# RWKV-7 and a GELU network in one kernel: turning the block inverses of two chunks on VectorE instead of through DRAM, with a new order of steps

## The chip, the cores and the metric

The kernel runs on one core of a Trainium2 chip. The metric is the device time of one execution in microseconds (us); a comparison uses the median of several runs. A profile is taken by the hardware profiler in an execution of its own. Its span is the time from the core's first to its last instruction.

## What is computed

Two parts follow each other. The first is a recurrence over 768 time steps, for 4 batches and 8 heads, each with a state of 40 x 40; the second is a two-layer network with the exact GELU on the 3072 x 320 rows that come out.

```python
# r, k, v, w, a, b: (4, 8, 768, 40) float32
for t in range(S):
    y[:, :, t] = einsum('bhd,bhde->bhe', rt, state)
    Sa = einsum('bhde,bhe->bhd', state, at)
    state = state * wt[:, :, None, :] - einsum('bhd,bhe->bhde', Sa, bt) + einsum('bhd,bhe->bhde', vt, kt)
x = y.transpose(0, 2, 1, 3).reshape(3072, 320)
h = x @ w_in                                  # w_in: (320, 2048), in 64-bit words
out = (0.5 * h * (1 + erf(h / sqrt(2)))) @ w_out   # w_out: (2048, 320), in 64-bit words
```

## The kernel before

**Chunks.** The 768 steps are cut into 12 chunks of 64 (c = 0 to 11). Inside a chunk the recurrence is written as matrix products, so that only one 64 x 64 triangular system per batch and head has to be inverted; the state is passed from chunk to chunk. The 32 pairs of batch and head lie on 128 partitions in pairs, 16 matrices side by side in the free dimension, two halves of 64 partitions, each of two blocks of 32.

**Steps and engines.** Every piece of work is a small function marked `@step`, named by two or three letters. The string in `order` lists all steps of all chunks in the order in which their instructions are issued; `perform` calls them one by one. There is no other scheduler: each engine executes its own instructions in just this order, and waits at one whose inputs are not there yet or whose target is still being read. So a step that waits holds up what stands behind it on its engine, and on SP's DMA queue too. The five engines are PE (TensorE), DVE (VectorE), ACT (ScalarE), POOL (GpSimd) and SP, which only issues DMAs.

**One chunk.** `Lw`, `La`, `Lb`, `Lk`, `LV`, `Lr` load the inputs (SP). `lg`, `wT`, `cu`, `ec`, `ew` form the cumulated decays; `ta`, `tb`, `tk`, `tr`, `tv` turn the inputs, on PE for chunks 0 to 2 and on DVE from chunk 3 on. `nm` (PE) and `nk` (DVE, line 839) make the strictly upper triangular matrices N; `vm`/`vk` and `am`/`ak` two further masked products. `av`, `xm`, `xc0`, `xc1` form the right-hand side, `sm` (PE) applies the inverse, `sc` masks it, `pk`, `pb` update state and output, `oa`, `om`, `od`, `oc`, `ot`, `tn` scale the state, turn it for the next chunk and write the network's input `xt`; `ox` moves rows of `xt` between partitions by DMA.

**The inverse.** For chunk 0 it is made of repeated squarings (`qt`, `qi`, `qm`, `qz`, `qb`, `qa`, `qc`, `ql`, `qx`), a chain between PE, DVE and ACT. For all other chunks the diagonal blocks of 32 x 32 (64 of them) are inverted on GpSimd by substitution, and then joined to the 64 x 64 inverse:

- `Ns` writes the blocks of N to DRAM, `Nl` reads them back so that each partition holds one whole block (1024 numbers in `Nb`), twice, once for each half of the partitions: one half solves the even rows of a block's inverse, the other the odd rows.
- `iz` sets `W` to rows of the identity, `ic.c.j0.j1` (lines 901 and 903) takes steps j0 to j1 of the substitution: a product into `tmp` and an addition to `W`, 62 instructions a chunk. Eight such steps make a solve.
- `Is` writes the inverses to DRAM, `If` reads them back as diagonal blocks into `Tt`, `Ij` some of them into `T2`.
- `tc_` (DVE, line 1001) turns them, `jm`, `jc`, `km`, `kt0`, `kt1` compute the block off the diagonal.

**The network.** `mh.c.p` (PE, line 1241) multiplies 256 rows of `xt` by 128 columns of the first weights, `ge` is the GELU, and the second product is made in one piece for chunk 0 (`pm`) and by seven half-size products with sums for the others (`m1` to `m7`, `s1` to `s4`, `e1` to `e6`, line 1280).

**The weights.** They come as 64-bit words (`Lf`, `Lf5`, `Ls`) and are made 32-bit numbers in 26 units u: 0 to 9 of 128 x 512 for `w_in`, 10 to 25 of 128 x 320 for `w_out`. `cp`, `cm`, `cs` (DVE) and `ce` (ACT) take exponent, mantissa and sign apart; the last step is either `cv` (two instructions on DVE, lines 612 and 613), or `cl` and `cn` (ACT, lines 620 and 627) with `cg` (two on GpSimd, lines 635 and 636), or, for unit 2 alone, `cx` (two matmuls on PE) with `cy`.

**Warm steps.** `warm` and `warm_first` are matmuls whose result nobody reads.

Of the kernel before, what the change touches and what calls it, by code (L numbers as in the profile page):

```python
# [16 lines left out]
def order(chunks, first_seven):  # L17
    return """
        pads_rows.0 Lw.0 sums_mask lg.0 pads_w.0 wT.0 of_half_set identity pads_r.0 ew.0 Lf.1.0.0 pads_r.1
        pads_extra.3 pads_VR.0 pads_a.0 cu.0 ec.0 Lk.0 pads_w.1 pads_a.1 bias_set pads_extra.0 first_ones.1  # L20
        first_ones.0 Tt_zero onward_set Lb.0 sb.0 La.0 warm.4.25 tb.0 pads_VR.1 sk.0.p pads_extra.2 upper_mask
        warm.4.14 tk.0 sn.0 ta.0 sa.0 warm_set warm.4.16 nm.0 nk.0 qt warm.4.5 Lf.3.1.0 Lf.1.1.0 Lf.0.0.0
        Lf.3.0.0 Lf5.0.1 Lf.0.0.1 cp.1 cm.1 Lw.1 La.1 ce.1 cs.1 qm.0 lg.1 qi.0.p pads_extra.1 qi.1.v qz.0
        qb.0.0.v cv.1 Lf.0.1.0 Lf.0.1.1 cu.1 qb.0.1.a qc.0 wT.1 ew.1 cm.3 cp.3 ce.3 ec.1 qm.1 qz.1 qb.1.1.a qc.1
        cp.0 ce.0 cl.3 cl.5 cn.3 Lr.0 Lb.1 Lf.2.1.1 Lf5.1.0 cs.3 qa.1 warm_first ta.1 qb.1.0.v sb.1 sa.1 kc.0
        qm.2 qz.2 cs.0 qb.2.0.v cm.0 tr.0 qc.2 rc.0 qa.2 cg.3 am.0 tb.1 qb.2.1.a cp.5 cv.0 cm.5 sn.1 qm.3 nm.1
        qz.3 nk.1 qa.3 qb.3.0.v ce.5 cn.5 Lf.1.1.1 LV.0 qb.3.1.a tv.0 Lf5.0.0 Lf.2.1.0 Lf.2.0.0 Lf.2.0.1 Lf5.1.1
        LV.1 Ns.1.1 Ns.1.0 Ls.0 Ls.1 Lf.1.0.1 Lr.1 Lk.1 cs.5 cm.2 cp.2 ak.0 qm.4 qa.4 cg.5 cp.7 ql vc.0 cl.7 cl.2
        vm.0 cn.2 cx.2 warm.4.11 vk.0 qc.3 ce.2 cs.2 cy.2 cp.4 ce.7 qx cm.4 cm.7 ce.4 cn.7 Ls.2 Lf.3.0.1 Lf.3.1.1
        Nl.1.0 Lw.2 Ls.4 Nl.1.1 av.0 jm.0 jc.0 km.0 xc1.0 cs.7 pads_rows.1 cg.7 cs.4 cv.4 cp.6 xc0.0 kt0.0 kt1.0  # L30
        ce.6 cm.6 cl.6 cn.6 cp.9 cm.9 tr.1 cs.6 ce.9 rc.1 sm.0 sc.0.1 cs.9 sc.0.0 cv.9 tv.1 pk.0 pb.0 cg.6 cp.8
        sk.1.v om.0.0 cm.8 od.0.1 od.0.0 om.0.1 ce.8 vc.1 cs.8 cv.8 cp.10 tk.1 kc.1 am.1 oc.0 ot.0.0 warm.4.15
        vm.1 ot.0.1 Ls.3 Ls.7 ce.10 lg.2 Lr.2 ox.0.1 Lb.2 La.2 tn.0 cm.10 cs.10 ak.1 cp.11 cv.10 wT.2 cu.2 ew.2
        ce.11 vk.1 cp.12 tr.2 ec.2 ce.12 rc.2 cs.11 cm.11 cv.11 cm.12 cs.12 cm.13 cp.13 cv.12 cp.14 cm.14 av.1
        ym.1 yc.1 sb.2 warm.4.1 xm.1 ta.2 ox.0.0 Ls.6 Ls.5 Ls.8 Ls.9 La.3 Lw.3 tb.2 ce.14 xc1.1 ce.13 sn.2 sa.2
        cs.14 cv.14 cs.13 cp.16 ce.16 cv.13 cp.15 ce.15 xc0.1 mh.0.2 nm.2 mh.0.6 cs.16 cm.16 cm.15 cs.15 cv.15
        cp.17 cm.17 nk.2 ce.17 cv.16 cp.18 ce.18 cs.17 cv.17 cp.19 ce.19 cs.18 cm.18 cm.19 Ls.11 LV.2 cs.19 cv.19
        mh.0.7 mh.0.4 mh.0.3 mh.0.0 ge.0.1 cp.21 ce.21 cm.21 cv.18 Ls.10 Ns.2.1 Ns.2.0 mh.0.1 tv.2 mh.0.5 iz.1
        ic.1.0.4 ic.1.4.8 ic.1.8.12 ic.1.12.16 ic.1.16.20 ic.1.20.24 ic.1.24.28 ic.1.28.31 unused.v unused.a
        Ls.13 Is.1.0.s Is.1.1.s Nl.2.0 Ls.15 Ls.12 Nl.2.1 iz.2 ic.2.0.4 ic.2.4.8 ic.2.8.12 ic.2.12.16 ic.2.16.20  # L40
# [1360 lines left out]
```

## Time and profile before

| what | value |
|---|---|
| median of 3 runs | 667.89 us (666.51 to 668.05) |
| the profiled execution | 671.35 us |
| its span | 669.6 us |
| mean granted clock of TensorE | 0.977 |
| instructions | 28037 |
| packets of DMA, bytes | 306133, 79.23 MB |

All shares and durations in the profile belong to the one profiled execution. A row of the timeline gives start, duration, engine, line, operation, what is written and read, the count, and in brackets the idle time before it with what ended it. A row of a group gives the busy time in us, the mean of one instruction in ns and the idle time before. PEclk is the granted clock of TensorE as a share of full speed.

### The profile page before, as it was taken

The page shows a single profiled execution, that of the slowest core. Times are in us where ns is not written, and L with a number is a line of the kernel's source. Part 1 is how long each engine was busy: PE and PEld are TensorE (multiplying, and loading weights), DVE is VectorE, ACT ScalarE, POOL GpSimd, SP SyncE. Part 2 cuts the span into 40 slices and gives each one's busy share as a digit, 9 for nine tenths or more (in the row PEclk, how much of TensorE's full clock was granted, in tenths as well). Part 3 has the DMA queues.
Part 4 walks back from the last instruction along what each step waited for, and adds up shares of the span by engine and source line. Part 5 has one row for each costly group of instructions (what it writes and reads, how often), then busy time and mean ns, then how long its engine had stood idle before and what let it go on. Part 6 is the DMA issues. An engine that isn't in the chain of part 4 may idle for free.

```text
span 669.6 us, 28037 instructions
## 1 busy us (share of the span) xinstructions
PE 632.3 (94%) x12416; PEld 556.7 (83%) x12416; DVE 449.6 (67%) x572; ACT 285.2 (43%) x388; POOL 390.1 (58%) x796
## 2 busy tenths in 40 slices
...
GB/s 149 169 162 180 134 154 192 155 110 111 160 117 100 171 83 143 153 106 164 142 81 147 160 111 114 158 99 122 165 102 132 108 85 131 14 81 9 28 14 20
DMA packets 306133, 79.23 MB, mean 118 GB/s; under 512 B 285628, under 2 KB 300892, under 8 KB 306012
## 3 DMA queue, kind: packets, MB, share of 16 engines
...
## 4 chain that ended last, share of the span: by engine, by line
PE 66%; POOL 13%; SPq 7%; DMA 6%; issue 4%; DVE 3%; ACT 1%; DVEq 0%; POOLq 0%; ACTq 0%
PE bank L1241 25%; PE bank L1280 22%; PE bank L197 18%; POOL W L903 7%; POOL tmp L901 7%; SPq L437 2%; SPq L560 2%; DMA inv_blocks<-W 1%; DMA w_out_sb<-in_moe_w_in_dram 1%; DMA Tt<-inv_blocks 1%; DMA Nb<-N_blocks 1%; SPq L880 1%; DMA SM<-in_w_dram 1%; SPq L527 1%; DMA N_blocks<-spare 1%
## 5 line engine op out<-in xcount | busy, mean ns | idle before, releaser
L1241 PE MATMUL bank<-xt,w_in_sb 64*128 64x256 f32 x1920 | 224.6, 386 | 0.0
L901 POOL TENSOR_TENSOR tmp<-W,Nb 128x126 f32<-128x126 f32 (+22 forms) x341 | 161.7, 474 | 91.5 <-DMA Nb<-N_blocks 56.6
L1241 PEld LDWEIGHTS bank<-xt,w_in_sb 64*128 64x128 f32 x1920 | 184.3, 190 | 24.1 <-issue 1.1
L903 POOL TENSOR_TENSOR W<-W,tmp 128x126 f32<-128x126 f32 (+22 forms) x341 | 165.5, 485 | 26.7
L1280 PE MATMUL bank<-w_out_sb,gt 128*128 128x160 f32 x704 | 102.1, 302 | 0.0
L1246 ACT ACTIVATE gt<-bank 128x1024 f32<-128x1024 f32 x48 | 48.9, 1024 | 122.5 <-PE bank L1241 120.8
L1280 PEld LDWEIGHTS bank<-w_out_sb,gt 128*128 128x128 f32 x704 | 96.6, 190 | 3.9 <-issue 2.6
L1109 DVE TENSOR_TENSOR SM<-bank,upper 128x832 f32<-128x832 f32 (+1 forms) x24 | 23.1, 989 | 20.1 <-PE bank L197 19.9
L1197 ACT COPY conv<-st 32x128 f32<-32x128 f32 (+2 forms) x55 | 28.0, 509 | 16.8 <-DVE st L1191 16.1
L1280 PE MATMUL bank<-extra,conv 128*128 128x160 f32 x208 | 30.4, 300 | 0.0
L1233 DVE TENSOR_TENSOR os<-os,bank 128x160 f32<-128x160 f32 x44 | 13.9, 315 | 23.5 <-PE bank L1280 16.1
L590 ACT ACTIVATE conv<-conv,rebias 128x320 uint32<-128x320 uint32 (+1 forms) x26 | 16.1, 622 | 30.5 <-DVE conv L583 30.3
L1280 PEld LDWEIGHTS bank<-extra,conv 128*128 128x128 f32 x208 | 28.8, 190 | 0.2
L1001 DVE STREAM_TRANSPOSE conv<-Tt 128x512 f32<-128x512 f32 x11 | 7.8, 710 | 31.3 <-DMA Tt<-inv_blocks 31.2
L1050 DVE COPY Tt<-bank 32x512 f32<-32x512 f32 x9 | 6.2, 689 | 33.6 <-ACT Tt L1050 33.6
L696 DVE TENSOR_TENSOR_SCAN kT<-spare,kT 128x256 f32<-128x256 f32 x36 | 24.7, 744 | 4.9 <-ACT kT L689 4.9
L1161 DVE TENSOR_TENSOR st<-bank,st 128x832 f32<-128x832 f32 (+1 forms) x22 | 21.0, 986 | 10.1 <-PE bank L197 10.1
L892 POOL MEMSET W<- 128x512 f32 x11 | 5.9, 537 | 36.7 <-DMA inv_blocks<-W 36.7
L1233 DVE TENSOR_TENSOR conv<-gt 128x1024 f32<-128x1024 f32 x11 | 14.0, 1276 | 19.6 <-ACT gt L1246 19.6
L197 PEld LDWEIGHTS bank<-SM,Tt 64*64 64x64 f32 x768 | 19.2, 140 | 8.6 <-issue 4.5
L1280 PE MATMUL bank<-extra,gt 128*128 128x160 f32 x176 | 26.0, 301 | 0.0
L197 PE MATMUL bank<-SM,Tt 64*64 64x104 f32 (+1 forms) x768 | 22.5, 261 | 3.5 <-ACT Tt L1050 1.2
...
## 6 DMA issues: line engine op xcount, KB each, us to landing
...
```

The lines of the kernel that those rows point to most:

```text
L197: nc.tensor.matmul(o, lhsT, rhs, start=first, stop=True, skip_group_check=True)
L590: nc.scalar.activation(power, power, ACT.Relu, bias=rebias, scale=8.0)
L696: nc.vector.tensor_tensor_scan(logs[:, at:at + n], onward, logs[:, at:at + n], 0.0, ALU.mult, ALU.add)
L901: nc.gpsimd.tensor_tensor(t, W[:, :rows, j:j + 1].to_broadcast([P, rows, rest]), Nb[:, j:j + 1, j + 1:].to_broadcast([P, rows, rest]), ALU ...
L903: nc.gpsimd.tensor_tensor(W[:, :rows, j + 1:], W[:, :rows, j + 1:], t, ALU.add)
L1109: nc.vector.tensor_tensor(SM[:, g, :, :, cols], pair_of(f"S{c}_", g).rearrange("p x i c -> p i x c")[:, :, :, cols], kept, ALU.mult)
L1161: nc.vector.tensor_tensor(to, pair_of(f"QY{c}_", g)[:, :, :, cols], to, ALU.add)
L1197: nc.scalar.copy(apart.rearrange("p e i g d -> p (e i g) d")[to_rows, :, to_col:to_col + n], st.rearrange("p e i g c -> p (e i g) c")[rows ...
L1233: nc.vector.tensor_tensor(to, one_, other, how)
L1241: nc.tensor.matmul(ph[:, x, s], w_in_sb[half(x), kt, p * P:(p + 1) * P], xt[half(x), kt], start=kt == 0, stop=kt == NK - 1)
L1246: nc.scalar.activation(gt[:, 4 * q:4 * q + 4].rearrange("p (x s) t -> p x s t", x=2), bank(f"ph{c}_{q}").rearrange("p x (s t) -> p x s t", ...
L1280: nc.tensor.matmul(po[:, n, :DM // 2], l_[:, f], r_[:, f], start=f == 0, stop=f == NF // 2 - 1)
```

## The change

For chunks 1 and 2 (c < NX = 3) the ten DMA steps `Ns`, `Nl`, `Is`, `If`, `Ij` are gone. In their place:

- `nd` (ACT) copies the lower blocks of N beside the upper ones, so that all four blocks stand in the same 32 columns.
- `nx` (DVE) turns N by 32 x 32 blocks straight into `Nb`, each number twice, for the two parities. Each partition then holds a whole block, but turned, and so `ic` solves from the last row up; its shapes stay the same.
- `iz` puts the identity's rows into `W` by copies from a small pattern `parity`, which `stripes_set` (GpSimd) and `parity_set` (DVE) make once.
- `wx` (DVE) turns `W` back into the second 32 columns of `Tt`; `wa` (ACT) copies two of the blocks to their place on the diagonal, `wb` (ACT) some to `T2`. `tc_` reads the second columns.

Chunks 3 to 11 keep the way through DRAM. All steps are put in a new order; `ic` is now spread between other steps. Read for each engine by itself, the new order has the same sequence as the old one from `sm.4` on. The last step of several weight units changes its engine, unit 2 included, and there are 13 `warm` steps for 9.

```diff
--- before
+++ after
...
+        stripes_set Lw.0 sums_mask parity_set warm_set warm_first pads_w.1 identity Lb.0 pads_a.0 first_ones.1
+        pads_rows.1 pads_w.0 onward_set La.0 pads_r.1 pads_extra.1 pads_r.0 first_ones.0 pads_extra.2 pads_VR.0
+        Lf.1.0.0 Tt_zero Lw.1 lg.0 warm.4.9 bias_set upper_mask cu.0 pads_a.1 Lf.0.0.0 of_half_set warm.4.12
+        Lf.0.1.0 pads_extra.0 ec.0 wT.0 Lf.1.1.0 sb.0 Lf.2.1.0 ew.0 Lf.2.0.0 ta.0 tb.0 sa.0 Lb.1 warm.4.7 sn.0
+        warm.4.11 nm.0 La.1 nk.0 lg.1 qt qi.0.p cu.1 Lf.3.0.0 qm.0 cp.1 Lf.1.0.1 cp.0 ce.1 cm.1 cm.0 ce.0 Lk.0
+        cs.0 cv.0 wT.1 ec.1 cl.2 cp.2 cn.1 cs.1 Lf.3.1.0 cl.1 qz.0 ce.2 qb.0.0.v cg.1 sb.1 ew.1 qi.1.v qc.0
+        Lf.2.0.1 qb.0.1.a cm.2 Lf5.0.1 ta.1 tb.1 sa.1 qm.1 sn.1 cn.2 sk.0.p Lr.0 nm.1 qz.1 cs.2 pads_extra.3
+        Lf5.0.0 tk.0 qa.1 cg.2 nk.1 qc.1 qb.1.1.a qb.1.0.v nd.1 cp.3 qm.2 kc.0 LV.0 nx.1 iz.1 ce.3 am.0 Lf.0.1.1
+        qz.2 ic.1.0.4 qa.2 warm.4.29 qb.2.1.a Lf5.1.1 qb.2.0.v qc.2 cm.3 qm.3 cp.4 ak.0 ce.4 Lf.0.0.1 ic.1.4.8
+        cl.4 cm.4 Lf.2.1.1 cs.3 tr.0 qa.3 warm.4.8 Lf.1.1.1 cs.4 rc.0 tv.0 qz.3 Lr.1 qb.3.0.v qb.3.1.a pads_VR.1
+        cv.3 cn.4 qc.3 qm.4 cg.4 Lw.2 vc.0 cp.5 vm.0 ce.5 qa.4 Ls.1 cm.5 warm.4.19 qx ql ic.1.8.12 Lf5.1.0
+        warm.4.22 cp.6 jm.0 vk.0 cs.5 jc.0 av.0 cm.6 cv.5 ce.6 km.0 ic.1.12.16 cp.7 warm.4.0 Lk.1 cm.7 ce.7 cs.6
+        tr.1 xc0.0 kt1.0 cs.7 kt0.0 rc.1 Ls.0 xc1.0 sm.0 cv.7 Lf.3.1.1 ic.1.16.20 cl.9 warm.4.26 Lf.3.0.1 cm.9
+        cp.9 LV.1 sc.0.1 pk.0 lg.2 ce.9 sk.1.v cu.2 Lb.2 cl.11 sc.0.0 cn.9 cv.6 pb.0 La.2 ec.2 cs.9 cg.9 tk.1
+        od.0.1 Lr.2 cp.8 warm.4.13 om.0.0 kc.1 wT.2 om.0.1 ic.1.20.24 ce.8 od.0.0 ox.0.1 cs.8 tv.1 ew.2 cm.8 cv.8
+        oc.0 am.1 vc.1 cm.10 ot.0.1 sb.2 cp.10 ot.0.0 ic.1.24.28 ta.2 cn.10 ce.10 tb.2 ox.0.0 sa.2 vm.1 tn.0 sn.2
+        cl.10 ic.1.28.31 nm.2 ak.1 Ls.2 tr.2 cm.11 cs.10 cg.10 nk.2 mh.0.0 Ls.7 cp.11 wx.1 ce.11 Ls.3 cn.11 vk.1
+        nd.2 rc.2 mh.0.2 Ls.5 cs.11 cg.11 cp.12 cm.12 ce.12 nx.2 Ls.4 wb.1 mh.0.1 iz.2 Ls.11 cs.12 ic.2.0.4 cv.12
+        av.1 Ls.9 ge.0.0 cp.13 cm.13 ce.13 Ls.6 ym.1 cl.15 cs.13 cv.13 mh.0.3 yc.1 LV.2 cm.15 cp.15 cm.14 cn.15
+        cp.14 Lk.2 mh.0.4 ce.15 ce.14 cs.15 cg.15 cl.21 cs.14 Ls.10 cl.16 cv.14 ge.0.1 mh.0.5 Ls.8 wa.1.0 cp.17
+        unused.v cp.16 ce.17 cm.16 wa.1.1 cm.17 unused.a xm.1 La.3 cs.17 cn.16 cv.17 ce.16 cp.19 cs.16 cg.16
+        pm.0.0 ce.19 cm.19 xc0.1 Ls.13 sk.2.v cs.19 cv.19 Ls.12 ic.2.4.8 cp.18 Ls.15 cp.21 ce.18 cm.18 cm.21
+        xc1.1 tk.2 cs.18 cv.18 Lr.3 cn.21 pm.0.1 kc.2 cm.20 ce.21 cp.20 cs.21 cg.21 ce.20 cn.20 ta.3 cl.20 Lbt.3
+        tv.2 cp.23 cs.20 cg.20 ce.23 cm.23 cl.22 cs.23 cv.23 mh.0.6 vc.2 Ls.14 cp.25 ic.2.8.12 cp.22 ce.25 cm.22
+        cm.25 Lw.3 ge.0.2 cs.25 mh.0.7 cv.25 ce.22 cn.22 tc_.1 vm.2 cs.22 unused.r Lwt.3 jm.1 vk.2 cg.22 jc.1
+        tr.3 ge.0.3 km.1 Lk.4 ic.2.12.16 cp.24 warm.4.17 kt1.1 tb.3 ce.24 am.2 Lkt.3 kt0.1 sm.1 ak.2 lg.3
+        warm.4.10 sc.1.1 La.4 cl.24 ic.2.16.20 sc.1.0 pk.1 cm.24 cs.24 cn.24 pb.1 Lk.3 tw.3 lt.3 oa.1.1 Lv.3
+        cg.24 pm.0.2 oa.1.0 od.1.1 om.1.1 om.1.0 ic.2.20.24 od.1.0 ox.1.1 pw.3 pm.0.3 oc.1 ot.1.1 ot.1.0 tn.1
+        ew.3 av.2 ic.2.24.28 pc.0.0 Lb.3 pc.0.1 en.3 tk.3 ym.2 ox.1.0 cu.3 sn.3 yc.2 xm.2 sa.3 ec.3 ic.2.28.31
+        tv.3 nm.3 xc1.2 mh.1.0 xc0.2 nk.3 kc.3 Ns.3.1 wx.2 vm.3 Ns.3.0 tc_.2 wb.2 iz.3 am.3 vk.3 so.0.1 sk.3.p
+        jm.2 ta.4 mh.1.1 Nl.3.0 jc.2 wa.2.0 Nl.3.1 Lbt.4 mh.1.6 ge.1.0 wa.2.1 Lr.4 km.2 ic.3.0.4 mh.1.7 kt1.2
+        kt0.2 Lwt.4 sm.2 ge.1.3 ic.3.4.8 mh.1.2 sc.2.1 Lw.4 sc.2.0 tr.4 mh.1.3 ic.3.8.12 so.0.0 tw.4 pk.2 ge.1.1
+        tb.4 Lv.4 pb.2 ak.3 ic.3.12.16 lt.4 mh.1.4 oa.2.1 LV.3 oa.2.0 od.2.0 mh.1.5 Lkt.4 od.2.1 ws.0 m1.1 ge.1.2
+        ic.3.16.20 La.5 oc.2 s1.1 ot.2.1 m2.1 om.2.0 ot.2.0 LV.4 om.2.1 tn.2 av.3 e1.1 ox.2.1 s2.1 ym.3
+        ic.3.20.24 ws.1 lg.4 m5.1 yc.3 s4.1 m6.1 tk.4 s3.1 Lr.5 xm.3 e3.1 ws.3 m3.1 e2.1 xc0.3 ox.2.0 xc1.3
+        ic.3.24.28 e4.1 sb.3 m7.1 tv.4 pw.4 Lwt.5 cu.4 vm.4 ic.3.28.31 mh.2.2 ew.4 e5.1 en.4 Is.3.0.p vk.4 ec.4
+        mh.2.3 Is.3.1.p sn.4 sa.4 mh.2.4 ge.2.1 ws.2 iz.4 If.3.0 mh.2.5 kc.4 sk.4.p Ij.3.0 ta.5 If.3.1 nm.4 Lb.4
+        am.4 nk.4 m4.1 tc_.3 Ns.4.0 tr.5 ge.2.2 Ns.4.1 jm.3 e6.1 tw.5 Ij.3.1 mh.2.6 jc.3 so.1.1 ak.4 lt.5 Nl.4.1
+        mh.2.7 Nl.4.0 pw.5 Lbt.5 km.3 ge.2.3 mh.2.0 kt1.3 sb.4 Lw.5 kt0.3 ic.4.0.4 sm.3 mh.2.1 sc.3.1 so.1.0
...
@@ -155,6 +156,7 @@
     NT = 3
     NB = 3
     NS = 1
+    NX = 3
 
     const = ctx.enter_context(tc.tile_pool(name="const", bufs=1))
     dram = ctx.enter_context(tc.tile_pool(name="scr", bufs=1, space=bass.MemoryType.DRAM))
@@ -232,6 +234,7 @@
     W_tile = tile_of("W", [P, BL // 2 * BL])
     tmp_tile = tile_of("tmp", [P, BL * BL // 7])
     T2 = tile_of("T2", [P, G * NP, BL])
+    parity = tile_of("parity", [P, 2, BL])
     Js_tile = tile_of("Js", [P, G * NP, BL])
     os_both = tile_of("os", [P, G, DM])
     N_blocks = [dram.tile([2, 2, NBL, BL, BL], FP32, name=f"N_blocks{i}") for i in range(2)]
@@ -396,6 +399,16 @@
     @step
     def bias_set():
         nc.gpsimd.memset(rebias, -896.0 * 2.0 ** 23)
+
+    @step
+    def stripes_set():
+        for x in range(2):
+            for y in range(2):
+                nc.gpsimd.memset(Js_tile[:, x, y::2], 1.0 if x == y else 0.0)
+
+    @step
+    def parity_set():
+        nc.vector.transpose(parity, Js_tile[:, :2])
 
     @step
     def of_half_set():
@@ -887,9 +900,42 @@
         blk = N_blocks[c % 2].rearrange("j z n s t -> (j z n) s t")
         engine(q).dma_start(out=Nb[half(par)], in_=blk)
 
+
+
+
+    @step
+    def nd(c):
+        N = flat(N_of(c))
+        for rows in hi:
+            nc.scalar.copy(N[rows, :, :BL], N[rows, :, BL:])
+
+    @step
+    def nx(c):
+        blocks = flat(N_of(c))[:, :, :BL].rearrange("p n t -> p t n")
+        nc.vector.transpose(Nb_tile.rearrange("p (t n q) -> p t n q", n=NBL, q=2),
+                            blocks.unsqueeze(3).to_broadcast([P, BL, NBL, 2]))
+
+    @step
+    def wx(c):
+        nc.vector.transpose(flat(Tt)[:, :, BL:].rearrange("p n (t q) -> p t n q", q=2),
+                            W_tile.rearrange("p (t n q) -> p t n q", n=NBL, q=2))
+
+    @step
+    def wa(c, x):
+        nc.scalar.copy(flat(Tt)[lo[x], :, :BL], flat(Tt)[lo[x], :, BL:])
+
+    @step
+    def wb(c):
+        for x in range(2):
+            nc.scalar.copy(T2[lo[x]], flat(Tt)[hi[x], 1::2, BL:])
+
     @step
     def iz(c):
         nc.gpsimd.memset(W, 0.0)
+        if c < NX:
+            for x in range(2):
+                nc.gpsimd.tensor_copy(W_tile[:, x::BL + 2], parity[:, x, :BL // 2])
+            return
         for par in range(2):
             nc.gpsimd.memset(W[half(par)].rearrange("p s t -> p (s t)")[:, par::BL + 2][:, :BL // 2], 1.0)
 
@@ -898,6 +944,12 @@
         for j in range(j0, j1):
             rows, rest = j // 2 + 1, BL - 1 - j
             t = tmp_tile[:, :rows * rest].rearrange("p (s t) -> p s t", s=rows)
+            if c < NX:
+                own = W[:, BL // 2 - rows:, :rest]
+                nc.gpsimd.tensor_tensor(t, W[:, BL // 2 - rows:, rest:rest + 1].to_broadcast([P, rows, rest]),
+                                        Nb[:, rest:rest + 1, :rest].to_broadcast([P, rows, rest]), ALU.mult)
+                nc.gpsimd.tensor_tensor(own, own, t, ALU.add)
+                continue
             nc.gpsimd.tensor_tensor(t, W[:, :rows, j:j + 1].to_broadcast([P, rows, rest]),
                                     Nb[:, j:j + 1, j + 1:].to_broadcast([P, rows, rest]), ALU.mult)
             nc.gpsimd.tensor_tensor(W[:, :rows, j + 1:], W[:, :rows, j + 1:], t, ALU.add)
@@ -998,7 +1050,7 @@
 
     @step
     def tc_(c):
-        nc.vector.transpose(L_tile, flat(Tt)[:, :, :BL])
+        nc.vector.transpose(L_tile, flat(Tt)[:, :, BL:] if c < NX else flat(Tt)[:, :, :BL])
 
     @step
     def jm(c):
```

154 lines of the change are left out of this document (58 added, 96 removed).

## The prediction

> **What bounds the kernel now.** I read the page first, then the busy time by stage, then the waits, then single rows of the timeline. The page's busy times and its chain that ended last:
>
> ```profile
> PE 632.3 (94%) x12416; PEld 556.7 (83%) x12416; DVE 449.6 (67%) x572; ACT 285.2 (43%) x388; POOL 390.1 (58%) x796
> ...
> PE 66%; POOL 13%; SPq 7%; DMA 6%; issue 4%; DVE 3%; ACT 1%; DVEq 0%; POOLq 0%; ACTq 0%
> ```
>
> TensorE is busy 94% of the span. A change that adds no matrix work can win only what PE loses: 669.6 - 632.3 = 37.3 us of idle time, some time at a lowered clock, and the matmuls of `warm`, which compute nothing. The view of busy time by stretches shows where that lies. I cut it at starts of PE steps: `nm.0` 18.9, `pb.0` 72.1, `sm.1` 127.2, `jm.3` 221.4, `sm.4` 278.8.
>
> ```profile
> core 0: us, PE busy (x) PEld busy (x) DVE busy (x) ACT busy (x) POOL busy (x), PEclk, DMA share, GB/s
> 0.00:18.90 18.90, 9.71 (x99) 6.72 (x100) 2.15 (x3) 6.05 (x6) 9.40 (x37) 1.00 1.03 156
> 18.90:72.10 53.20, 45.80 (x1138) 36.30 (x1142) 43.07 (x65) 30.91 (x45) 15.11 (x16) 0.84 0.92 169
> 72.10:127.20 55.10, 49.92 (x980) 39.94 (x970) 48.70 (x97) 30.95 (x44) 35.88 (x87) 1.00 0.80 159
> 127.20:221.40 94.20, 85.95 (x1774) 73.99 (x1775) 70.74 (x79) 42.59 (x55) 63.94 (x116) 0.97 0.66 121
> 221.40:278.80 57.40, 56.16 (x1148) 49.92 (x1148) 41.42 (x48) 19.77 (x28) 41.49 (x92) 0.95 0.77 138
> 278.80:669.60 390.80, 384.79 (x7294) 349.83 (x7292) 243.52 (x285) 154.88 (x210) 224.32 (x449) 1.00 0.56 100
> ```
>
> PE's idle time (length less PE busy) is 9.2, 7.4, 5.2, 8.3 and 1.2 us in the first five stages, 31.3 in sum, and 6.0 in the last. The two orders in the diff, read engine by engine, are identical from `sm.4` on. So I let the last 390.8 us stand and price only the stages before. In the third stage DVE is nearly as full (48.7 of 55.1) as PE (49.9): there a saving on PE alone is worth little.
>
> What the change goes for is seen in the waits (total, times, longest), and in the rows of chunk 1's blocks: made by `nk.1` (DVE) at 45.43, first used by GpSimd's `ic.1` at 72.88.
>
> ```profile
> POOL tmp L901 <- DMA Nb<-N_blocks: 56.6, 7, 16.7
> ```
>
> ```profile
> 45.43 1.23 DVE L839 TENSOR_TENSOR spare<-bank,upper 128x1024 f32<-128x1024 f32 x1 [0.18 <-PE bank L197]
> ```
>
> ```profile
> 72.88 0.24 POOL L901 TENSOR_TENSOR tmp<-W,Nb 128x31 f32<-128x31 f32 x1 [3.07 <-issue]
> ```
>
> These 56.6 us are waits of GpSimd, not of PE; PE has other steps meanwhile. Only PE's own gaps count below.
>
> **The change part by part.**
>
> *The moved blocks.* Out go, for chunks 1 and 2, `Ns`, `Nl`, `Is`, `If`, `Ij`, all on SP's queue; the weight loads and chunk loads behind them there (`Lw.2`, `Ls`) no longer stand behind a landing. In come `nd` (ACT, 2 copies), `nx` (DVE, one turn), `wx` (DVE, a half-size turn), `wa` and `wb` (ACT, 2 copies each). The rows of like work:
>
> ```profile
> L1212 DVE STREAM_TRANSPOSE turned<-conv 128x1024 f32<-128x1024 f32 x11 | 13.5, 1227 | 0.9 <-ACT conv L1197 0.9
> L1001 DVE STREAM_TRANSPOSE conv<-Tt 128x512 f32<-128x512 f32 x11 | 7.8, 710 | 31.3 <-DMA Tt<-inv_blocks 31.2
> L627 ACT ACTIVATE conv<-conv 128x512 f32<-128x512 uint32 x5 | 3.1, 623 | 0.6 <-DVE conv L597 0.6
> L635 POOL TENSOR_TENSOR conv<-conv,gt 128x512 f32<-128x512 f32 x3 | 4.3, 1420 | 17.1 <-ACT conv L627 17.1
> ```
>
> DVE gets 2 x (1.23 + 0.71) = 3.9 us, ACT at most 12 x 0.62 = 7.4 us. `nx` reads with steps of 256 bytes and each element twice; no row shows such a read, so it lies between 1.23 and, read twice, 2.46 us. I take 1.23: the elements written are as many. It cannot be cheaper than a plain turn of that size. The Trainium skill, page "SBUF — State Buffer", note on cachelines in "SBUF: two separate sides", says that each access crossing to another 16-byte line pays a penalty, which would put `nx` nearer the upper end; the sum below would then be -7.6 instead of -10.0 us, with both turns on the path. No run here shows it.
>
> `ic` keeps its 62 instructions a chunk and their sizes, mirrored: no cost, and none saved. `iz` swaps two small memsets for two small copies: nothing either way. The set-up (`stripes_set`, `parity_set`) lies in the first 7 us, under the wait for the first load.
>
> *The conversions.* Units 1, 4, 9, 10, 11, 15, 16, 20, 21, 22, 24 go from `cv` (DVE) to `cl`, `cn` (ACT) and `cg` (GpSimd), units 3, 5, 6, 7 the other way, and unit 2 loses its two matmuls on PE (`cx.2`). The four and the three of the larger units with `cy.2` about cancel; eight small ones leave DVE. The same groups, from a stretch with GpSimd at work (84 to 104) and, the second row, from one where it rests (104.6 to 119):
>
> ```profile
> L597 DVE TENSOR_SCALAR conv<-w_out_sb 128x320 uint32<-128x320 uint32 x7 | 3.6, 525 | 0.0
> ```
>
> ```profile
> L597 DVE TENSOR_SCALAR conv<-gt 128x320 uint32<-128x320 uint32 x3 | 1.0, 325 | 0.0
> ```
>
> ```profile
> L612 DVE SCALAR_TENSOR_TENSOR conv<-w_out_sb,conv 128x320 f32<-128x320 uint32 x6 | 3.9, 650 | 0.0
> L613 DVE SCALAR_TENSOR_TENSOR w_out_sb<-conv 128x320 f32<-128x320 f32 x6 | 3.4, 568 | 0.2
> ```
>
> A `cv` is 0.65 + 0.57 = 1.2 us, so eight are 9.8 us off DVE, six of them in stage three. Against that, GpSimd now works through nearly all of that stage, so the later units, which ran beside a resting GpSimd, pay the first row's price: 0.2 us for each of `cp`, `cm`, and I take as much for `cs`, on eight units: 8 x 0.6 = 4.8 us. GpSimd gets 8 x 2 x 1.42 x 320/512 = 14.2 us, ACT at most 8 x 2 x 0.62 = 10 us on an engine with 24 us free in that stage.
>
> *The order, stage by stage.* First the rows of PE's early steps:
>
> ```profile
> 7.69 1.99 PE L197 MATMUL bank<-cum_m,w_tile 64*64 64x64 f32 x64 [7.69 <-ACT w_tile L660]
> ...
> 18.89 1.16 PE L197 MATMUL bank<-aT,nT 40*64 40x64 f32 x64 [0.62 <-DVE aT L748]
> ...
> 33.13 2.84 PE L197 MATMUL bank<-w_in_sb 128*128 128x512 f32 x6
> ...
> 52.49 1.88 PE L197 MATMUL bank<-conv,ident 128*128 128x512 f32 x2
> 54.17 1.91 PE L197 MATMUL bank<-w_out_sb,ident 128*128 128x512 f32 x2
> 55.88 1.15 PE L197 MATMUL bank<-cum_m,ident 128*128 128x512 f32 x2
> ```
>
> Stage 1. `warm_first` (2.84) moves into the 7.69 us in which PE waits for the first load; `Lb.0` and `La.0` are issued right behind `Lw.0`; `cu.0` comes ahead of `wT.0` (1.99), so `sb.0` and `tb.0` start about 2 us sooner; `tk.0` leaves the stage. Between 0 and -4 us; I take **-2.5**.
>
> Stage 2. Gone from PE: `cx.2`, 55.88 - 52.49 = 3.4, and `warm_first`, 2.7. Added: six `warm` steps for two, 4 x 1.15 = 4.6; they stand where PE would wait, and half of that I count as time. `nd.1` and `nx.1` stand in ACT's and DVE's queues ahead of `kc.0` and `qz.2`, which chunk 0's chain of squarings waits for: 1.2 + 1.2, of which I count 1.3. So -3.4 - 2.7 + 2.3 + 1.3 = **-2.5**. Bounds: -6 with the added steps all in gaps, +2 with none of it won (the chain of squarings then waiting for DVE as before).
>
> Stage 3. DVE: six `cv` -7.2, `wx.1` and `nx.2` +1.9, contention +4.8; about as before, so the stage keeps its 55.1. But PE does more in it: `tv.1`, `tk.2`, `am.2` for `cu.2`, together some 3 us that no longer lie elsewhere, in the 5.2 us idle. I take **-2.5**, bounds -6 and +7 (rivals).
>
> Stage 4. Chunk 2's round trip goes, and what PE idled behind it; chunk 3 still goes through DRAM:
>
> ```profile
> 171.84 2.75 PE L197 MATMUL bank<-SM,extra 64*64 64x104 f32 x61 [1.94 <-issue]
> ...
> 221.41 1.08 PE L197 MATMUL bank<-conv,spare 32*32 32x32 f32 x64 [4.33 <-DVE conv L1001]
> ```
>
> The first gap, 1.94, and some of the time at half clock behind it (PEclk 0.97) go: **-2.5**. The 4.33 at `jm.3` stay: from `nm.3` to `jm.3` PE has the same steps in both orders, and the chain `Ns.3`, `Nl.3`, `ic.3`, `Is.3`, `If.3` is as long. Bounds 0 and -8. Stage 5: 0. What is late next is this wait at `jm.3`.
>
> Sum: -2.5 x 4 = -10.0. The profiled execution took 671.35 (span 669.6), the median of the runs is 667.89, 0.5% lower; I take the difference off the median: 667.9 - 10.0 = **657.9 us**.
>
> **Rivals.**
>
> *GpSimd ends last (slower).* Solve 2 now shares GpSimd's queue with the `cg` steps. Solves took, chunk 1, 2, 3:
>
> ```profile
> 72.90:104.60 31.70, 26.83 (x617) 22.18 (x608) 30.45 (x53) 18.80 (x29) 26.91 (x62) 1.00 0.70 141
> 119.50:152.50 33.00, 31.80 (x683) 24.11 (x681) 27.86 (x37) 15.80 (x23) 28.18 (x62) 1.00 0.69 129
> 172.30:212.70 40.40, 40.36 (x736) 36.50 (x729) 35.88 (x37) 19.25 (x26) 35.62 (x62) 0.96 0.70 125
> ```
>
> `nm.1` now follows `qm.1`, so I put `ic.1` at 36; 31.7 and two large `cg` (2 x 2.8) end it at 73, before DVE reaches `wx.1`, which its order has some 15 us of DVE steps behind `sc.0.0` (63 at the earliest, so 78). `ic.2` from 81 with 33.0 and six small `cg` (1.8 each) ends at 125; PE wants it about 18 us after `sm.1` (121), at 139. With 40.4 for the solve, and each `cg` held up to 4.8 us between its two operations by ACT and DVE, eight of them from 75 on, it ends at 81 + 40 + 8 x 4.8 = 159, 20 us late. Half-way to that, ten late, cancels the gain; past it the kernel is slower. At 16 late: 667.9 - 10 + 16 = 674. Chance 0.17.
>
> *DVE becomes the bound in stage three.* Beside one `cg` operation DVE's small step stretched:
>
> ```profile
> 48.38 1.35 POOL L636 TENSOR_TENSOR w_in_sb<-conv 128x512 f32<-128x512 f32 x1 [2.15 <-DVE conv L604]
> ```
>
> ```profile
> 48.50 1.63 DVE L583 TENSOR_SCALAR conv<-w_out_sb 128x512 uint32<-128x512 uint32 x1
> ```
>
> It ended with it. If each of some 12 `cg` operations in that stage holds DVE 0.6 us (half a small operation's 0.9, and some), 7 us come on top: 667.9 - 10 + 7 = 665. Chance 0.19. By the Trainium skill, page "SBUF — State Buffer", section "SBUF: two separate sides", the two engines share a port pair that one of them holds for a whole instruction while the other is blocked; taken at full length this is that rival, and the trace shows it in these rows.
>
> *Chunk 3 comes early too.* With SP free of `If.2`, `Ij.2`, the 4.33 and its half clock go, and more of stages 2 and 3: 667.9 - 17 = 651. Chance 0.13.
>
> *Nothing is won:* the gaps only move, as loads set them: 667.9. Chance 0.07.
>
> **Numbers.** The forecast has 0.44. A measurement of this kernel can tell about 0.3% (2 us). Faster: 0.44 + 0.19 + 0.13 = 0.76; same 0.07; slower 0.17. The range runs from 647 (-4, -6, -6 and -5 in the four stages, all inside their bounds) to 670; that takes in the DVE case and no change, and leaves out most of the slower case and a little of the fast end.
>
> **What would show it.** Right: `ic.1` starting before 40; no matmul `conv,ident` on PE; `sm.1` near 121, `jm.3` near 208, `sm.4` near 269; turns of 1.2 us; the last stage again near 391. Wrong: a DVE wait at `wx` for L903, or a wait of `jm.2` for it; `cp` and `cm` near 1 us; more half clock before 120; a last stage that differs by over 2 us.

## The result and the profile after

Over 20 executions of each, the changed kernel took 662.05 us (656.05 to 666.87), the kernel before 666.63 us (662.49 to 670.13): a ratio of 0.992, with a 95% interval of 0.9895 to 0.9945. Run again beside other kernels it had 0.9888 (0.9844 to 0.9932). So it is faster by about 1%: 0.8 and 1.1% in the two measurements, with intervals that run from 0.5 to 1.6%. The two profiled executions, 671.35 and 658.18 us, lie above and below their kernels' medians, so the difference of the two traces, 13.2 us, is more than twice the 4.6 us between the medians.

Busy time and the chain that ended last, from the page of the changed kernel:

```profile
PE 627.9 (96%) x12420; PEld 552.4 (84%) x12420; DVE 455.0 (69%) x562; ACT 298.0 (45%) x414; POOL 400.4 (61%) x816
...
PE 49%; POOL 20%; DMA 10%; SPq 7%; DVE 6%; issue 5%; ACT 2%; POOLq 0%; DVEq 0%; ACTq 0%
```

Busy time by stretches of the changed kernel, cut at the starts of the same steps (`nm.0`, `pb.0`, `sm.1`, `jm.3`, `sm.4`):

```profile
0.00:14.30 14.30, 12.36 (x99) 6.66 (x100) 2.78 (x4) 6.64 (x7) 7.06 (x39) 1.00 0.95 151
14.30:66.60 52.30, 41.60 (x1117) 33.17 (x1116) 46.46 (x63) 33.52 (x48) 32.93 (x54) 0.93 1.02 169
66.60:128.50 61.90, 54.95 (x1072) 44.88 (x1076) 54.78 (x90) 40.51 (x65) 44.67 (x83) 0.92 0.69 150
128.50:208.40 79.90, 79.63 (x1690) 68.76 (x1682) 65.84 (x72) 40.01 (x56) 52.64 (x100) 1.00 0.67 118
208.40:267.30 58.90, 55.70 (x1166) 49.92 (x1165) 41.03 (x49) 22.41 (x31) 39.79 (x92) 1.00 0.70 127
267.30:656.40 389.10, 383.70 (x7294) 348.99 (x7292) 244.06 (x285) 154.94 (x210) 223.27 (x451) 1.00 0.56 101
```

Against before the stages differ by -4.6, -0.9, +6.8, -14.3, +1.5 and -1.7 us. The third is much longer. In the fourth, PE's idle time (length less PE busy) fell from 8.3 to 0.3 us; the rest is 84 matmuls fewer (the third stage has 92 more) and the clock (0.97 before, 1.00 now). The joins of chunk 2 (`jm.2`) and chunk 3 (`jm.3`) had stood behind 0.58 and 4.33 us of idle time; now both stand without an idle time in brackets. PE's timeline at `jm.2` before, then at `jm.2` and `jm.3` of the changed kernel:

```profile
162.37 0.75 PE L197 MATMUL bank<-conv,N 32*32 32x32 f32 x64 [0.58 <-DVE conv L1001]
```

```profile
153.94 0.75 PE L199 MATMUL bank<-conv,N 32*32 32x32 f32 x64
...
208.42 0.75 PE L199 MATMUL bank<-conv,spare 32*32 32x32 f32 x64
```

The 1.94 us of before stand elsewhere: 9 us behind `jm.2`, inside `pb.2`, between its first three matmuls and the other 61, and what ended them is "issue". So the trace doesn't show that PE waited there for the round trip. In the changed kernel `pb.2` runs without a pause (169.8 to 171.4 us).

In the third stage PE now waits for VectorE above all. Its three longest waits from 62 to 132 us (total, times, longest); a fourth, 0.4 us, is for ScalarE, and in the same stage of the kernel before it waited 1.6 us for VectorE, at `sb.2`, and 3.2 for ScalarE. Line 1053 is `tc_.1`, 772 `sb.2`, 852 the masked copies, here `vk.2`:

```profile
PE bank L199 <- DVE conv L1053: 2.6, 1, 2.6
PE bank L739 <- DVE extra L772: 2.1, 1, 2.1
PE bank L199 <- DVE VR L852: 1.9, 1, 1.9
```

What was asked of single steps is seen in GpSimd's and VectorE's timelines: `ic.1` starts at 38.1 instead of 72.9, and the turns cost what plain turns cost.

```profile
38.08 0.24 POOL L949 TENSOR_TENSOR tmp<-W,Nb 128x31 f32<-128x31 f32 x1 [1.22 <-DVE Nb L915]
```

```profile
36.71 1.23 DVE L915 STREAM_TRANSPOSE Nb<-spare 128x1024 f32<-128x1024 f32 x1
...
84.45 0.70 DVE L920 STREAM_TRANSPOSE Tt<-W 128x512 f32<-128x512 f32 x1
```

### The profile page after: what moved, and what is told of

Its sections match the earlier page's. It is cut to its first block, busy times and chain, and to the rows that moved or that the text cites. A ratio compares the mean times of both kernels' runs of the same rounds, so it can differ in the third digit from the quotient of the medians.

```text
span 656.4 us, 28104 instructions
## 1 busy us (share of the span) xinstructions
PE 627.9 (96%) x12420; PEld 552.4 (84%) x12420; DVE 455.0 (69%) x562; ACT 298.0 (45%) x414; POOL 400.4 (61%) x816
## 4 chain that ended last, share of the span: by engine, by line
PE 49%; POOL 20%; DMA 10%; SPq 7%; DVE 6%; issue 5%; ACT 2%; POOLq 0%; DVEq 0%; ACTq 0%
PE bank L1293 16%; PE bank L1332 16%; PE bank L199 15%; POOL tmp L953 10%; POOL W L955 9%; DMA inv_blocks<-W 4%; SPq L450 3%; PE bank L1414 2%; DMA Nb<-N_blocks 2%; SPq L540 1%; DMA r_pairs<-in_r_dram 1%; SPq L967 1%; DVE conv L617 1%; DMA w_out_sb<-in_moe_w_in_dram 1%; SPq L893 1%
## 5 line engine op out<-in xcount | busy, mean ns | idle before, releaser
L1293 PE MATMUL bank<-xt,w_in_sb 64*128 64x256 f32 x1920 | 220.5, 381 | 1.7 <-DVE late L852 1.5
L1293 PEld LDWEIGHTS bank<-xt,w_in_sb 64*128 64x128 f32 x1920 | 181.7, 187 | 24.7 <-DVE late L852 1.7
L955 POOL TENSOR_TENSOR W<-W,tmp 128x126 f32<-128x126 f32 (+22 forms) x279 | 131.5, 471 | 21.9
L951 POOL TENSOR_TENSOR W<-W,tmp 128x126 f32<-128x126 f32 (+22 forms) x62 | 29.5, 476 | 4.9
L1102 DVE COPY Tt<-bank 32x512 f32<-32x512 f32 x9 | 6.2, 689 | 27.3 <-ACT Tt L1102 27.3
L1332 PEld LDWEIGHTS bank<-extra,gt 128*128 128x128 f32 x176 | 24.4, 190 | 0.2
```

The lines of the kernel that those rows point to most:

```text
L951: nc.gpsimd.tensor_tensor(own, own, t, ALU.add)
L955: nc.gpsimd.tensor_tensor(W[:, :rows, j + 1:], W[:, :rows, j + 1:], t, ALU.add)
L1293: nc.tensor.matmul(ph[:, x, s], w_in_sb[half(x), kt, p * P:(p + 1) * P], xt[half(x), kt], start=kt == 0, stop=kt == NK - 1)
L1332: nc.tensor.matmul(po[:, n, :DM // 2], l_[:, f], r_[:, f], start=f == 0, stop=f == NF // 2 - 1)
```

## The experiments

The theory: the turns take two round trips out of the chain and, by emptying SP's queue, bring chunk 3 forward; the third stage is as long as VectorE's list and gives a part back. The rivals: GpSimd's `cg` steps hold VectorE up; the turns alone or the order alone do the work; the idle time only moves.

Starts of steps and lengths in each trace (us), and each kernel's ratio to before with its interval:

```
kernel                       ratio                     pb.0..sm.1  sm.1..jm.3  sm.4 at
before                       1                            55.1        94.2      278.8
old order, turns (fixed)     0.9983 [0.9952, 1.0014]      55.6        88.4      277.0
old order, Ns.3 early        0.9957 [0.9926, 0.9988]      55.6        92.1      273.4
old order, unit 2            1.0002 [0.9975, 1.0029]      55.0        96.1      279.1
new order, both via DRAM     1.0151 [1.0102, 1.0199]      64.4        87.2      284.3
new order, chunk 1 turned    1.0055 [1.0025, 1.0086]      65.7        85.9      279.9
changed kernel               0.992  [0.9895, 0.9945]      61.9        80.0      267.3
changed kernel again         0.9888 [0.9844, 0.9932]      58.8        81.6      270.0
  with cv for cg             0.9971 [0.9938, 1.0005]      62.4        80.4      271.4
  without the small cg       0.9915 [0.9878, 0.9952]      60.8        80.1      272.2
  tc_.1 early                0.9915 [0.9885, 0.9946]      58.1        81.9      271.0
  without warm6              0.9900 [0.9866, 0.9935]
  without 14 cs              0.9822 [0.9761, 0.9882]      53.2        80.3      263.0
```

**The turns without the order.** The old order and conversions, with the round trips of chunks 1 and 2 replaced.

```diff
-Ns.1.1 Ns.1.0 ... Ns.2.1 Ns.2.0 ... Is.1.0.s Is.1.1.s ... If.1.1 If.1.0 Ij.1.0 Ij.1.1 ...
+nd.1 nx.1 ... nd.2 nx.2 ... wx.1 wa.1.0 wa.1.1 wb.1 ...
```

> Old order and old conversions, with only the way of the blocks changed for chunks 1 and 2: nd, nx, wx, wa, wb stand where Ns, Is, If, Ij stood, stripes_set and parity_set at the start. Theory (the turn pays only with an order that uses it): the solve of chunk 1 stays behind the cg steps on GpSimd's queue and starts near 70 instead of 72.9; the solve of chunk 2 loses its two waits; PE wins only the gaps behind chunk 2's blocks: -2 us, ratio 0.997 (0.993 to 1.000). Rival (the turn alone is the gain): -5 us, ratio 0.992, as the change itself.

Measured: 1.0353 (1.0305 to 1.0401), neither. The edit was badly placed: `nx.2` stood where chunk 2's stores had stood, ahead of `ic.1` in the list, so the first chunk was solved with the second one's blocks, after waiting for them. GpSimd's waits from 60 to 140 us and VectorE's from 95 to 140:

```profile
POOL tmp L942 <- DVE Nb L908: 39.0, 1, 39.0
```

```profile
DVE Tt L913 <- POOL W L944: 27.3, 1, 27.3
```

So this run says nothing on the theories, but shows the price of a step at the wrong place of an in-order queue: VectorE stands 27.3 us at `wx.1`, and the weight conversions behind it stand too. With `nx.2` behind `wx.1`:

```diff
-nd.2 nx.2 iz.1 ic.1.0.4 ... wx.1 wa.1.0 wa.1.1 wb.1 Ls.15 Ls.12 iz.2
+nd.2 iz.1 ic.1.0.4 ... wx.1 wa.1.0 wa.1.1 wb.1 nx.2 Ls.15 Ls.12 iz.2
```

> The old order and the old conversions with the turns in place of the round trips for chunks 1 and 2, as in turn_old_order, where however the second chunk's turn into the shared tile stood ahead of the first chunk's solve, so that GpSimd waited 39.0 us for it and the first chunk was solved with the second one's blocks. Here nx.2 stands behind wx.1. Theory A: the 23 us were that misplacement; the turns alone then take away the 1.94 us wait at chunk 2's join and a part of chunk 3's 4.33 us, for 3.9 us more on VectorE: ratio 0.993 to 1.004. Theory B: in the old order the turns hold VectorE's queue (wx.1 has to wait there for GpSimd's solve, which starts at 67 us, with weight conversions queued behind): ratio 1.010 to 1.030, with a wait of VectorE at wx.1 or nx.2 of over 5 us.

Measured: 0.9983 (0.9952 to 1.0014), theory A. `sm.1` comes 3.6 us later than before and `jm.3` 2.2 us earlier. Of the 3.6 us, 3.1 are there at `pb.0` already, when of the 3.9 us of turns only `nx.1` has been put on VectorE; what makes the rest is not shown. The wait at `jm.2` is gone. PE's timeline at `pb.2` and `jm.3`, where before had 1.94 and 4.33:

```profile
173.97 1.64 PE L192 MATMUL bank<-SM,extra 64*64 64x104 f32 x59 [1.04 <-issue]
219.16 0.74 PE L192 MATMUL bank<-conv,spare 32*32 32x32 f32 x64 [1.58 <-DVE conv L1046]
```

In the old order what is won at the joins is lost before `sm.1`. The pause inside `pb.2` is still there, at 1.04 us and without a round trip, which speaks against the round trip as its cause.

**The order without the turns.** New order and conversions, both chunks through DRAM (`NX = 0`), and with chunk 1 alone turned (`NX = 2`). The stores `Is` are issued on GpSimd's queue here (`.p`), in the kernel before on SP's (`.s`).

```diff
-    NX = 3
+    NX = 0
-nd.1 ... nx.1 ... wx.1 ... nd.2 ... nx.2 ... wx.2
+Ns.1.1 Ns.1.0 ... Nl.1.0 Nl.1.1 ... Is.1.0.p Is.1.1.p ... Ns.2.1 Ns.2.0 ... Nl.2.0 Nl.2.1 ... Is.2.0.p Is.2.1.p
```

> The new order and conversions, but the blocks of chunks 1 and 2 go through DRAM as before (Ns and Nl where nd and nx stood, Is behind the last ic on GpSimd's queue, If and Ij where wa and wb stood). Theory: ic.1 starts some 15 us later than the 34.4 of the changed kernel, holds cg.4 and cg.9 behind it and with them the first mh steps; DVE and PE wait: +3 to +10 us against before, ratio 1.005 to 1.015. Rival (the order and the lost matmuls of unit 2 are the gain, the turn is not needed): ratio 0.992.

> The changed kernel's order and conversions, chunk 1 by turns, chunk 2 through DRAM. With both through DRAM the ratio was 1.015, with both turned 0.992. If each turn is worth its own round trip, this lies halfway, 1.001 to 1.006, and jm.2 and jm.3 start 5 to 8 us later than the changed kernel's 153.9 and 208.4 while sm.1 stays near 128.5. If the first turn carries nearly all (it frees the shared tiles and the queue early), 0.992 to 0.996; if the second does, 1.010 or more.

Measured: 1.0151 and 1.0055. The order, with the round trips put where the turns stood, makes the kernel slower, by the upper end of what was expected; another place for them was not tried. Chunk 1's turn then wins 1.0%, chunk 2's another 1.4 to 1.7%, so each is worth about its own round trip. That jm.2 and jm.3 would start 5 to 8 us later held, nearly (161.0 and 217.2, 7.1 and 8.8 later); that `sm.1` would stay near 128.5 did not: 131.3. With chunk 2 through DRAM, PE waits at its join again (from 145 to 180 us, kernel with chunk 1 turned):

```profile
PE bank L194 <- DVE conv L1048: 3.8, 1, 3.8
```

With both through DRAM the conversions wait for weights, whose loads stand behind the blocks on SP's queue; VectorE's longest wait for a DMA in the third stage of that kernel (71 to 136 us):

```profile
DVE conv L605 <- DMA w_out_sb<-in_moe_w_out_dram: 3.3, 1, 3.3
```

So the parts don't add: the turns alone nothing that can be told, the order alone 1.5% lost, together 0.8 to 1.1% won.

**Why chunk 3's wait went.** In the kernel before, GpSimd's waits from 145 to 180 us (line 901 is `ic.3`, 892 `iz.3`); then the same view of the changed kernel:

```profile
POOL tmp L901 <- DMA Nb<-N_blocks: 11.8, 1, 11.8
POOL W L892 <- DMA inv_blocks<-W: 5.5, 1, 5.5
```

```profile
POOL W L934 <- DVE Tt L920: 5.2, 1, 5.2
POOL tmp L953 <- DMA Nb<-N_blocks: 5.0, 1, 5.0
```

Before, `Ns.3` was issued behind `If.2`, which waited for `Is.2` to land, and `ic.3` started 17.0 us behind `nk.3`; now 10.5. Whether it was the queue can be tried in the old kernel by moving a few DMA steps of chunks 2 and 3:

```diff
-... If.2.0 Ij.2.0 If.2.1 ... nk.3 ... Ns.3.1 Ij.2.1 Ns.3.0 ... Lbt.4 ... Nl.3.0 Nl.3.1
+... nk.3 Ns.3.1 Ns.3.0 If.2.0 Ij.2.0 If.2.1 ... Ij.2.1 Nl.3.0 Nl.3.1 ... Lbt.4
```

> The kernel before with five DMA steps of chunk 3 in another place in SP's queue and nothing else: its blocks' stores (Ns.3) ahead of chunk 2's loads If.2, Ij.2, and its reloads (Nl.3) ahead of Lbt.4. Theory: chunk 3 is late in the kernel before because its stores queue behind chunk 2's round trip, so the turns win at chunk 3's join, not only at chunk 2's. Then ic.3 starts 5 to 7 us earlier behind nk.3 (before: 17.1 us behind it, changed kernel: 10.5), the 4.33 us wait at jm.3 goes, jm.2 may wait up to 1 us longer, and the ratio is 0.993 to 0.997. Rival, as in the prediction: the wait at jm.3 is set by the chain's own length and stays near 4.3 us; ratio 0.999 to 1.002.

Measured: 0.9957 (0.9926 to 0.9988). GpSimd's waits from 145 to 180 us and PE's timeline:

```profile
POOL tmp L896 <- DMA Nb<-N_blocks: 8.4, 1, 8.4
POOL W L887 <- DMA inv_blocks<-W: 4.6, 1, 4.6
```

```profile
165.27 1.08 PE L192 MATMUL bank<-conv,N 32*32 32x32 f32 x64 [4.25 <-DVE conv L996]
...
218.76 0.75 PE L192 MATMUL bank<-conv,spare 32*32 32x32 f32 x64
```

The theory held in kind, not in size: `ic.3` is 14.3 us behind `nk.3` (a gain of 2.7 where 5 to 7 were expected), and the wait at `jm.3` is gone, but the one at `jm.2` grew from 0.58 to 4.25 us, as chunk 2's loads now queue behind chunk 3's stores. SP's timeline shows why the gain is small: the first store of `Ns.3` is issued 5.2 us behind the start of `nk.3` before, 3.8 here, since the loads of `Lv.3` still stand ahead of it, and 1.3 in the changed kernel. Queue order trades one wait for the other and keeps 0.4%; the turns in the new order remove both.

**What sets the third stage.** First GpSimd's part: the eight small units go back to `cv` on VectorE, or lose `cg` altogether for one copy on ScalarE.

```diff
-cl.10 cn.10 cg.10
+cv.10          (and units 11, 15, 16, 20, 21, 22, 24)
```

> The changed kernel with the eight small units 10, 11, 15, 16, 20, 21, 22, 24 ended by cv on DVE again instead of cl, cn and cg. Theory (what a cg takes off DVE it gives back by stretching DVE's operations beside it): DVE gets 8 x 1.0 us of cv and loses about as much stretching; within 2 us of the changed kernel, ratio 0.989 to 0.995. Rival (DVE's load is the sum of its own unstretched steps, and DVE bounds the stage before sm.1): +8 us against the changed kernel, ratio 1.004.

```diff
+        if u >= 2 * NK:
+            nc.scalar.copy(to, mant_f)
+            return
         nc.gpsimd.tensor_tensor(mant_f, mant_f, lo.bitcast(FP32), ALU.add)
```

> The changed kernel with one ACT copy of 128x320 in place of the two GpSimd operations of cg for the eight small units; the sum with the low word and the factor of the power are left out, so these weights are not the reference's. Theory (DVE is the bound from 67 to 121 and is stretched there by GpSimd's cg operations): 14 operations stop holding DVE for 0.4 to 0.7 us each, sm.1 comes 5 to 8 us sooner than 128.5, the kernel 4 to 6 us faster than the changed one, ratio 0.983 to 0.986. Rival (DVE is full of its own work, GpSimd costs it nothing): the same as the changed kernel, ratio 0.992.

Measured: 0.9971 (0.9938 to 1.0005), between the two; and 0.9915 (0.9878 to 0.9952), as the changed kernel. The third stage without `cg`:

```profile
70.50:131.30 60.80, 55.33 (x1068) 45.31 (x1072) 54.13 (x90) 42.22 (x71) 41.00 (x93) 0.92 0.62 139
```

So nothing is won by taking `cg` out. But this doesn't show that contention costs nothing: VectorE's busy time is 54.1 us, where the changed kernel's two traces have 54.8 and 52.8, and GpSimd is still busy 41.0 us, because the instructions of `ic.2` move forward into the gaps that `cg` leaves (`ic.2` ends at 124.5 instead of 147.6). VectorE's small steps stay stretched beside them: the two-input step `cs` takes 600 ns on average on `w_out_sb`, 628 in the changed kernel. What the stage would take beside a resting GpSimd was not tried. Next, PE's three waits: `sb.2`, `tc_.1` and `vk.2` earlier on VectorE.

```diff
-ox.0.1 cs.8 ... cm.10 ot.0.1 sb.2 ... cs.23 cv.23 mh.0.6 ... mh.0.7 cv.25 ce.22 cn.22 tc_.1 vm.2 cs.22 ... jm.1 vk.2
+ox.0.1 sb.2 cs.8 ... cs.23 cv.23 tc_.1 mh.0.6 ... cp.22 cm.22 ge.0.2 vm.2 jm.1 vk.2 jc.1 Lw.3 mh.0.7 cp.25 ...
```

> The changed kernel with three places of VectorE's list put earlier: the negated b of chunk 2 (sb.2) ahead of cs.8, and tc_.1 directly after cv.23, with vm.2 and jm.1 ahead of mh.0.7 on TensorE, unit 25 behind them, vk.2 ahead of unit 25. Theory: stage 3 is as long as VectorE's list makes it; TensorE's three waits there (2.09, 2.55 and 1.89 us) go, sm.1 starts 4 to 6 us earlier after pb.0 than in the changed kernel (57 us behind pb.0 against 61.9), and the kernel is 4 to 5 us faster than the changed one (ratio 0.984 to 0.987 to before where the changed one has 0.992). Rival: GpSimd's chain stands behind it; ic.2 ends at 147.6 us whatever VectorE does, so jm.2 and then jm.3 wait, and 3 us or more of the gain are given back there (ratio within 0.003 of the changed kernel's), with a wait of TensorE over 2 us at jm.2 or jm.3.

> The changed kernel once more, unaltered, so that the next kernels have it on the same chip and its stages have a second trace. If the two profiled runs overstated the change (the one of before lay 4.7 us above its median, the one of after 3.9 us under its own), the ratio is again 0.990 to 0.995 and the profiled span lies above 656.4 us with a granted clock under 0.987, the stages that lengthen being those with a clock under 1.00. If the traces told the truth and the medians were unlucky, 0.980 to 0.986.

Measured: 0.9915 (0.9885 to 0.9946) with the steps earlier, 0.9888 (0.9844 to 0.9932) for the changed kernel on the same chip: nothing won. The repeated kernel lies between its two cases, and its profiled span, 658.9 us at a granted clock of 0.976, is as the first of them had it. The rival's outcome held, but not by its reason: no wait over 2 us came up at `jm.2` or `jm.3`. PE's waits from 67 to 153 us, first of the kernel with the early steps, then of the changed kernel again:

```profile
PE bank L194 <- ACT nT L784: 1.6, 1, 1.6
PE bank L194 <- ACT Tt L1097: 1.5, 1, 1.5
PE bank L194 <- ACT gt L1293: 1.5, 1, 1.5
```

```profile
PE bank L199 <- DVE conv L1053: 1.6, 1, 1.6
PE bank L199 <- DVE VR L852: 1.6, 1, 1.6
PE bank L1414 <- POOL w_out_sb L649: 0.7, 1, 0.7
```

The waits have changed their names, from VectorE to ScalarE; their sum is no smaller. Moving steps within VectorE's list didn't shorten the stage. So the last run takes work out of VectorE's list:

```diff
-cs.10 cs.11 ... cs.23
```

> The changed kernel without VectorE's step cs of the units 10 to 23 (14 instructions, 0.48 to 1.17 us each in its trace, 9.7 us in sum; the weights of those units lose their sign, the rest is computed as before). Theory: VectorE's list sets the third stage, so pb.0 to sm.1 shrinks from 61.9 us to 54 to 57 and the kernel gets 3 to 6 us faster than the changed one (ratio 0.981 to 0.986, where the changed one has 0.989 to 0.992). Rival: TensorE with its granted clock and ScalarE's queue (which holds ce behind ge) set the stage; VectorE only waits instead, the stage shrinks by under 2 us and the ratio stays at 0.988 to 0.992.

Measured: 0.9822 (0.9761 to 0.9882), as the theory had it, though the interval still touches that of the changed kernel measured again. The stage is 53.2 us long, shorter than in the kernel before, with the granted clock at 1.00. The third stage by stretches: the changed kernel again, `cv` for `cg`, and without `cs`:

```profile
67.80:126.60 58.80, 53.99 (x1073) 43.84 (x1076) 52.83 (x88) 40.42 (x65) 44.11 (x82) 0.94 0.70 152
```

```profile
67.50:129.90 62.40, 53.71 (x1069) 43.17 (x1072) 59.16 (x102) 34.71 (x51) 41.62 (x93) 0.95 0.68 142
```

```profile
67.60:120.80 53.20, 51.55 (x1072) 42.47 (x1074) 47.08 (x74) 38.82 (x64) 41.78 (x79) 1.00 0.71 158
```

PE does the same matmuls in all three (1069 to 1073). The length follows VectorE's busy time: in the order `cv` for `cg`, changed kernel, without `cs`, 59.2, 52.8 and 47.1 us of it give 62.4, 58.8 and 53.2 us, and PE's waits for VectorE in the stage add up to 7.5, 3.8 and 1.4 us. Of the last 5.6 us, 2.4 are the clock, by PE's busy time; 3.2 are idle time of PE that went. So VectorE's list sets the length of the stage in the changed kernel; without `cs` PE, busy 51.6 of 53.2 us, is itself nearly full. It is the list with its waits, not the busy time alone: the two kernels with round trips have 53.6 and 54.3 us of VectorE's work, and stages of 64.4 and 65.7 us, in which VectorE waits 7.4 and 8.4 us for weights and for the other engines. And one trace of a kernel says little about 3 us: the changed kernel's own two differ by that much here (61.9 and 58.8).

**Two small terms of the sum.**

```diff
-cx.2 ... cy.2
+cg.2           (kernel before)
```

> The kernel before with weight unit 2 converted by ScalarE and GpSimd (cg.2), as in the changed kernel, in place of two matmul groups on TensorE and one step of VectorE (cx.2, cy.2). The prediction took 3.4 us off TensorE's path for this. Theory: TensorE is the bound in that stage, nm.0 to pb.0 gets 2.5 to 3.5 us shorter and the ratio is 0.994 to 0.997. Rival: loads and VectorE set the stage's length, the gap only moves: ratio 0.999 to 1.002.

```diff
-warm.4.29 ... warm.4.8 ... warm.4.19 ... warm.4.22 ... warm.4.0 ... warm.4.26      (changed kernel)
```

> The changed kernel without six idle matmul steps of the second stage (warm.4.29, 8, 19, 22, 0 and 26; they compute nothing). The prediction counted 2.3 us for the added ones. Theory: they stand on TensorE's path there and could go: 1.5 to 3 us faster than the changed kernel (ratio 0.984 to 0.987). Rival: they fill waits and hold the granted clock up; without them the clock from 15 to 60 us falls under the 0.89 to 1.00 seen, and the time stays the same or grows by up to 3 us (ratio 0.989 to 0.995).

Measured: 1.0002 (0.9975 to 1.0029) and 0.990 (0.9866 to 0.9935). Neither is worth anything that can be told. In the one trace without `cx.2` the stage from `nm.0` to `pb.0` is 1.9 us shorter than before (51.3 for 53.2, at a granted clock of 0.90 for 0.84), where 2.5 to 3.5 were expected, and this is lost again behind it: PE waits 2.90 us at `jm.2`, where before had 0.58, and `sm.4` starts at the same time. The gap moved, as the rival had it. Inside the stage, too, PE waits longer for VectorE and ScalarE a few us later (timeline of the old kernel with `cg.2`; before had 0.73 at the second of these and none shown at the first):

```profile
54.48 1.66 PE L192 MATMUL bank<-VR,nT 64*64 64x104 f32 x64 [1.41 <-DVE VR L834]
58.92 0.24 PE L192 MATMUL bank<-turned 32*32 32x32 f32 x2 [1.65 <-ACT turned L1017]
```

For the `warm` steps no trace shows the clock at the kernel's usual time, so whether they hold it up stays open. The times show that the six cost no more than some 2 us, which is as fine as these intervals go.

## Why the prediction was right, and where it was wrong

657.9 us was forecast, 662.05 came, inside the range; the direction and the reason (round trips out of PE's path) were right. The size was not: 10.0 us of gain were forecast, and 4.6 came, or 7.5 by the second ratio. The range reached from 647 to 670 and held "no change" too, so lying inside it says little. And the single stages missed by more than the sum: that their errors offset each other is luck.

- *Stage 1* (-2.5, bound -4): -4.6 in the first trace, -4.1 in the second, just past the bound. The mechanism was right (PE waits 1.9 us at the start instead of 7.7), the size too small.
- *Stage 2* (-2.5): -0.9 and -0.2. The step that failed is "gone from PE: `cx.2`, 3.4": taken out alone it shortened the stage by 1.9 us in one trace and the kernel by nothing. The +2.3 for idle matmuls was not found either, though the runs are too coarse to exclude it. I counted PE's instructions in a stage that is not filled by PE (45.8 of 53.2). What bounds it stays open: of PE's 10.7 us of idle time in the first trace of the changed kernel, 6.2 end with "issue", 3.9 are waits for VectorE and 0.2 for a load.
- *Stage 3* (VectorE's list "keeps its 55.1", -2.5 taken): 61.9 and 58.8, and `sm.1` at 128.5 and 126.6 instead of near 121. Conversions with their contention were about right (VectorE spent 36.1 us on units 10 to 25 between `pb.0` and `tc_.1` before and 33.2 after, and -2.4 was forecast). What was not counted are the other steps in VectorE's list: 12.9 us before, 21.0 after. The turns, 1.9, had been reckoned with; 5.0 more are 128 x 512 conversions of units 6, 8 and 9, whose ends the new order puts behind `pb.0` (2.6 us before, 7.6 after). The prediction let the large units cancel as a sum and didn't ask in which stage they lie. The first two stages bring PE to `pb.0` 5.5 us earlier, but VectorE comes to unit 10 only 2.4 us earlier (75.9 for 78.2) and to `tc_.1` at the same time (120.2 and 120.3). PE ran ahead of VectorE, and stood. That is the outcome of the second rival: with its 7 us on top of the -2.5 the stage would be 4.5 us longer than before, and it is 6.8 and 3.7. The rival's reason is not shown: `cg` steps do hold VectorE, but without them `ic.2` holds it as long, and nothing was gained.
- *Stage 4* (-2.5, "the 4.33 at `jm.3` stay"): from `sm.1` to `jm.3` the sum gives 91.7 us, while the starts named as signs, 121 and 208, give 87 and don't follow from it; 80.0 and 81.6 came. The step that failed is that the chain of chunk 3 "is as long": it is 6.5 us shorter from `nk.3` to `ic.3`, as its stores no longer queue behind chunk 2's loads on SP. That is the first part of the third rival, at 0.13. And the 1.94 us that were to go are a pause inside `pb.2` that no row ties to the round trip.
- *Stages 5 and 6* (0): +1.5 and -1.7, and +4.4 and -1.9 in the second trace. `sm.4` at 267.3 and 270.0 was forecast near 269. What is late next is not `jm.3` but chunk 4's join: PE waits there 1.31 and 2.53 us, before not at all.
- *GpSimd ends last* did not come: `ic.2` ends at 147.6, between the 125 of the sum and the 159 of the rival, and PE, itself late, does not wait at `jm.2`. The 4.8 us between the two operations of a `cg`, with which the rival reckons, stand in no row of before; the longest there is 2.15.
- *`nx`* took 1.23 us, the lower end. By the Trainium skill, page "SBUF — State Buffer", section "SBUF: two separate sides", a penalty per 16-byte line was possible; the trace shows none: the same instruction on a plain layout takes 1.227. But the same note has two hits on a line run at full bandwidth, and `nx` reads each number twice in a row, so this row does not test the penalty; the prediction overlooked that half of the note.
